# Attention decode step with a gated GLU: the last row of wo in two column halves, with the closing sums on GpSimd and VectorE

## The chip, the cores and the metric

The kernel runs on one core of a Trainium2 chip. The metric is the device time of one execution in microseconds. The engines are TensorE (PE in the profile; PEld is its weight load), VectorE (DVE), ScalarE (ACT), GpSimd (POOL) and SyncE (SP, which here only issues transfers). Sixteen DMA engines move data between the main memory (HBM) and the on-chip memory SBUF. TensorE writes its results to PSUM, from which VectorE and ScalarE read.

## The reference

One token `x` of 512 numbers is normalised. It then goes two ways: through attention over a cache of 8192 positions with 32 heads of 128 numbers, and through a gated unit whose silu is multiplied onto the attention's result. Everything is float32. Cut to what matters:

```python
# A: D = 512, H = 32, Sk = 8192, Dh = 128;  B: F = 1376
xn = layernorm(x)
q = (xn @ wq).reshape(1, 1, H, Dh)
p = softmax(einsum("bhqd,bhkd->bhqk", q, k_cache) * Dh ** -0.5)
s = einsum("bhqk,bhkd->bhqd", p, v_cache) -> (1, 1, H * Dh) @ wo      # wo: 4096 x 512
h = sigmoid(xn @ w_gate) * (xn @ w_up)
g = silu(h @ w_down)
out = x + s * g
```

The two caches hold 128 MB each (in units of 2 to the 20th), wq and wo 8 MB each.

## The kernel before

**Main part.** The 32 heads are worked off as 16 pairs. SP loads the keys of a pair (8 MB) into one of two slots in turn and the values into a third slot. VectorE multiplies the keys by the query in place (L415) and sums them to scores (L416). TensorE finds the largest score with ScalarE's and VectorE's help, ScalarE takes the exponentials (L430), and TensorE multiplies them by the values. Its instructions for one pair are recorded in a list by the class `Later` and played in a loop; each of them has the line L38 in the profile, so they are told apart by their tiles. The order on each engine is the order in which the program is written, with explicit semaphores: `wait(engine, step)` puts a wait ahead of the engine's next instruction, and `pe`, `dve`, `act` and `pool` count an engine's finished steps.

**Start.** VectorE clears `x_row` (L239). ScalarE's queue loads `x` into it (L240), 128 numbers on each of the partitions 0, 32, 64 and 96; these are the four groups (`NG` = 4, `GC` = 128 columns to a group). From `x_row` VectorE makes the normalised `xn`. GpSimd sets up constants with a few memsets and one select (L244 to L251), and clears a rest of w_down's place later (L323); after that it has nothing to do.

**Gate.** `column_sums` (L327) sums the rows of the gated unit's result over all partitions by matmuls with a column of ones. Each matmul puts 128 columns on the first partition of one group. ScalarE takes the sigmoid into `g_row` (L373). In the second turn of the pairs' loop VectorE multiplies `g_row` by the sum itself (L458), which completes silu.

**End.** `wo` is loaded by SP in nine pieces of rows (`W_ENDS`, L483; the profile names the line of the helper, L168). Row r of the 32 stands for 128 of the 4096 rows of wo, one on each partition, so a piece of one row is 128 runs of 2 KB. The rows are shared out as follows:

- rows in `W_DVE`: VectorE multiplies each by its column of `o_all`, the attention's output, and adds them into two partial sums (L513, L515), then adds those (L518);
- rows in `W_PE`: TensorE multiplies them into the bank `big[0]`, and VectorE adds this to its own sum, into `s_tmp` (`to_fold`, L490);
- rows 28 to 31 (`direct`): TensorE multiplies each, as soon as it has landed, in four matmuls of 128 columns into `acc`, one for each group of partitions. Ahead of row 31 it also sums `s_tmp` over the partitions into the same place (`fold`).

A matmul in float32 leaves two matmul records and two weight loads in the profile. At last VectorE multiplies `g_row` by `acc` (L537) and adds `x_row` (L539), and SP stores the four groups, 512 bytes each (L562), clears the semaphores and waits for the store to land.

## Time and profile before

| | |
|---|---|
| median of 3 runs | 684.65 us (684.42 to 684.74) |
| the profiled execution | 684.69 us |
| its span, first to last instruction | 683.3 us |
| mean granted TensorE clock | 0.67 |
| data read from HBM | 293.67 MB, 430 GB/s over the span |

How to read the profile: the page begins with the span and each engine's busy time and share. Then come rows with one digit for each of 40 equal slices of the span (9 is 90% busy or more). A row of an engine's groups has line, engine, operation, output<-inputs, shapes and count, then the busy time in us and the mean ns of one, then the engine's idle time before them in us and what ended it. In the timeline a row has start, length in us, engine and operation, and in brackets the idle time before it and what ended that; several instructions in a row are merged (x4), and the length is then from the first one's start to the last one's end. The chain of waits has start, length and what ran. A row for a DMA queue has its packets, the MB they moved and the share of the sixteen engines' time. SPq and ACTq are the engines' own queues, where they issue transfers.

### The profile page before, as it was taken

Reading aid. Unit: us, or ns where it says so; the run is one execution under the profiler, and the core shown is the slowest. Engines: PE = TensorE matmul, PEld = TensorE weight load, DVE = VectorE, ACT = ScalarE, POOL = GpSimd, SP = SyncE. Lnnn points to the kernel's source line nnn. Section 1 sums busy time; section 2 is a strip of 40 time slices with the busy share of each in tenths; the row PEclk is TensorE's granted clock in tenths of the full one; section 3 lists DMA queues with packets and bytes.
Section 4 is the critical chain, followed back from the end, with each engine's and each line's share of the span. In section 5 each row is a group of like instructions: output and inputs, shape, how many; then the busy total and the mean of one; then the engine's idle time right before and its main releaser. Section 6 shows DMA issues by size and latency. Waiting matters only on the chain. (4 is left out here: it accounts for less than half of the span.)

```text
span 683.3 us, 3400 instructions
## 1 busy us (share of the span) xinstructions
PE 218.8 (32%) x1376; PEld 62.3 (9%) x1376; DVE 616.0 (90%) x156; ACT 44.6 (7%) x142; POOL 2.6 (0%) x11
## 2 busy tenths in 40 slices
PE   0363025050503305050512306060512406060665
PEld 0120001010100101010100101010100101010110
DVE  3869999999999999998989899898989999999917
ACT  2040010000000100000010100000010101000010
POOL 0000000000000000000000000000000000000000
PEclk9987557575755757575665757575665757575897
DMA  9999999999999999999999999999999999999997
GB/s 382 429 440 460 437 434 430 430 430 430 430 430 430 430 430 430 460 441 445 434 430 430 430 430 430 430 430 430 430 437 437 460 430 403 472 399 430 435 430 331
DMA packets 7552, 293.67 MB, mean 430 GB/s; under 512 B 856, under 2 KB 864, under 8 KB 1664
## 3 DMA queue, kind: packets, MB, share of 16 engines
q1 hardware_dynamic: 7544, 293.67, 99.5%
q10 hardware_dynamic: 8, 0.00, 0.0%
HBM read 293.67 MB, written 0.00 MB: 430 GB/s over the span
## 5 line engine op out<-in xcount | busy, mean ns | idle before, releaser
L415 DVE TENSOR_TENSOR slot<-slot,q_all 128x16384 f32<-128x16384 f32 (+3 forms) x19 | 275.9, 14520 | 19.9 <-DMA slot<-in_A_k_cache_dram 19.9
L416 DVE TENSOR_REDUCE sc<-slot 128x128 f32<-128x16384 f32 (+3 forms) x19 | 276.0, 14525 | 0.7
L38 PE MATMUL psum<-slot,zeros 128*8 128x512 f32 x1024 | 148.5, 739 | 253.6 <-PEq L38 253.6
L38 PEld LDWEIGHTS psum<-slot,zeros 128*8 128x8 f32 x1024 | 30.3, 103 | 358.2 <-issue 358.2
L38 PE MATMUL psum<-ident,mx 128*1 128x128 f32 x32 | 8.4, 360 | 114.3 <-PEq L38 114.3
L437 ACT COPY o<-psum 128x512 f32<-128x512 f32 x16 | 9.4, 586 | 400.1 <-PE psum L38 400.1
L38 PE MATMUL psum<-slot,ones 128*128 (+3 forms) x36 | 17.7, 668 | 22.1 <-PEq L38 16.6
L290 DVE SCALAR_TENSOR_TENSOR slot<-slot,xn 128x1376 f32<-128x1376 f32 (+1 forms) x8 | 18.9, 2360 | 3.0 <-DMA slot<-in_A_wq_dram 2.7
L38 PE MATMUL psum<-o,pick 128*2 128x128 f32 x128 | 16.5, 272 | 12.8 <-PEq L38 12.8
L423 DVE STREAM_TRANSPOSE psum<-psum 32x128 f32<-32x128 f32 x16 | 5.0, 310 | 11.1 <-PE psum L38 11.1
L428 ACT ACTIVATE nb<-psum 128x2 f32<-128x2 f32 x16 | 2.8, 172 | 156.1 <-PE psum L38 156.1
L430 ACT ACTIVATE zeros<-sc,nb 64x128 f32<-64x128 f32 x32 | 12.8, 399 | 0.9
L38 PEld LDWEIGHTS psum<-ident,mx 128*1 128x1 f32 x32 | 1.8, 80 | 118.4 <-issue 118.3
L38 PEld LDWEIGHTS psum<-o,pick 128*2 128x2 f32 x128 | 9.9, 84 | 29.6 <-issue 27.2
L38 PE MATMUL psum<-slot,o_all 128*1 128x128 f32 (+1 forms) x54 | 9.5, 463 | 6.5 <-DMA slot<-in_A_wo_dram 6.5
L38 PE MATMUL psum<-zeros,rs 128*32 128x2 f32 x32 | 3.7, 187 | 23.5 <-PEq L38 23.5
L408 DVE TENSOR_REDUCE mx<-psum 1x2 f32<-1x128 f32 x16 | 4.4, 277 | 7.5 <-PE psum L38 7.5
L38 PE MATMUL psum<-mx,ones 1*128 1x2 f32 x32 | 8.2, 324 | 7.4 <-PEq L38 7.4
L515 DVE SCALAR_TENSOR_TENSOR q_all<-slot,o_all,q_all 128x512 f32<-128x512 f32 x15 | 10.0, 747 | 0.0
L38 PEld LDWEIGHTS psum<-slot,ones 128*128 128x128 f32 (+1 forms) x36 | 7.0, 218 | 32.5 <-issue 24.7
L38 PE MATMUL psum<-slot,o 128*1 128x512 f32 x26 | 5.0, 827 | 11.2 <-DMA slot<-in_B_w_down_dram 11.2
L38 PEld LDWEIGHTS psum<-mx,ones 1*128 1x128 f32 x32 | 7.3, 282 | 14.0 <-issue 14.0
(54 smaller groups left out, 61.3 us busy)
## 6 DMA issues: line engine op xcount, KB each, us to landing
slot<-in_A_k_cache_dram SPq DMA_DIRECT2D x2, 6144.0 KB, 37.9
slot<-in_A_v_cache_dram SPq DMA_DIRECT2D x3, 4096.0 KB, 23.0
slot<-in_A_wq_dram SPq DMA_DIRECT2D x2, 4096.0 KB, 16.6
slot<-in_A_k_cache_dram SPq DMA_DIRECT2D x2, 4096.0 KB, 40.5
slot<-in_A_k_cache_dram SPq DMA_DIRECT2D x2, 2048.0 KB, 42.4
slot<-in_B_w_gate_dram SPq DMA_DIRECT2D x1, 2752.0 KB, 26.9
slot<-in_B_w_up_dram SPq DMA_DIRECT2D x1, 2752.0 KB, 33.0
slot<-in_B_w_down_dram SPq DMA_DIRECT2D x1, 2560.0 KB, 22.7
```

The source lines that it names most:

```text
L38: ins = getattr(self.engine, name)(*args, **kwargs)
L290: return dve(DVE.scalar_tensor_tensor(y, w[:, k, cols], xn[:, k:k + 1], y, op0=ALU.mult, op1=ALU.add))
L408: DVE.reduce_max(mx[:1, 1:3], pt[0:1, :].rearrange("o (e p) -> o e p", e=2), axis=AX.X).then_inc(reduced, 1)
L415: wait(DVE, dve(DVE.tensor_mul(k[:, j, :], k[:, j, :], qb[:, i:i + 1, :].to_broadcast([P, n, Dh]))))
L416: summed[i] = dve(DVE.reduce_sum(sc[i % 2][:, j], k[:, j, :], axis=AX.X))
L423: turned_out[i] = dve(DVE.transpose(o, pn.rearrange("e (a r) -> e a r", r=WR)))
L428: wait(ACT, act(ACT.mul(nb, pm[:, :2], -SCALE)))
L430: ACT.activation(weights[h, :, e * HT:(e + 1) * HT], sc[i % 2][h].rearrange("p (g b) -> p g b", b=HT), AF.Exp, bias=nb[h, e:e + 1], scale= ...
L437: ACT.copy(o1, po).then_inc(copied, 1)
L515: ins = DVE.scalar_tensor_tensor(part[n], wo_t[:, r, :], col, part[n], op0=ALU.mult, op1=ALU.add)
```

## The change

The last row of wo, row 31, is loaded as two transfers of 256 columns each (128 runs of 1 KB), so there are ten pieces. All products of the rows 28 to 31 and of `s_tmp` are made by halves: eight matmuls of 64 columns in place of four of 128, into two banks, `acc[0]` and `acc[1]`. TensorE waits for each half of row 31 by itself. A group's 128 columns are now 64 of the first half of the result and 64 of the second. For that the gate's sums (`column_sums`), the stored result and a second load of `x` follow the new order. This second load goes into a new tile `x_add`, cleared at the start by VectorE and loaded on ScalarE's queue in the second turn of the pairs' loop; `x_row` stays as it was for the normalisation. VectorE multiplies the gate by the first half's product and GpSimd adds `x_add`; of the second half VectorE does both. SP waits for GpSimd and for VectorE, and stores eight runs of 256 bytes. There are two semaphores more.

```diff
--- before.py
+++ after.py
@@ -93,7 +93,7 @@
     W_DVE = [r for r in range(W_FOLD) if r not in W_PE]
     V_CUTS, K_CUTS = (NB // 2, NB * 13 // 16), {NP - 3: (NB * 3 // 4,), NP - 2: (NB * 3 // 4,), NP - 1: (NB // 2,)}
 
-    N_SEMS = 40
+    N_SEMS = 42
     DVE, ACT, SP, POOL = nc.vector, nc.scalar, nc.sync, nc.gpsimd
     PE = Later(nc.tensor)
     pe_only = OrderedEngineSet([nc.tensor.engine])
@@ -116,7 +116,7 @@
 
     pick = sb("pick", 2 * HT)
     slots = [sb(f"slot{i}", SLOT) for i in range(3)]
-    x_row, g_row = sb("x_row", GC), sb("g_row", GC)
+    x_row, g_row, x_add = sb("x_row", GC), sb("g_row", GC), sb("x_add", GC)
     ones, ident = sb("ones", P), sb("ident", P)
 
 
@@ -138,7 +138,8 @@
     psum = bank("psum", P, NK * QT)
     banks = [psum[:, i * QT:(i + 1) * QT] for i in range(NK)]
     big, po, wide = banks[:2], banks[2], banks[3:]
-    acc, pt, o_t = wide[0][:, :GC], wide[1][:, :P], wide[2][:GP, :H * WP + Dh]
+    pt, o_t = wide[1][:, :P], wide[2][:GP, :H * WP + Dh]
+    acc = [wide[n][:, :GC // 2] for n in range(2)]
     pm, pn = wide[3][:, :4], wide[4][:GP, :Dh]
 
 
@@ -238,6 +239,7 @@
 
     c_xrow = dve(DVE.memset(x_row, 0.0))
     ld_xr = load(ACT, "xr", x_row[0:P:GP, :], xv.rearrange("(g c) -> g c", g=NG), c_xrow)
+    c_xadd = dve(DVE.memset(x_add, 0.0))
     ACT.nop().then_inc(q_free, NK)
     ACT.nop().then_inc(s_val[1], 16 * (NP - 2))
     ACT.nop().then_inc(s_val[2], 16 * (NP - 1))
@@ -326,7 +328,8 @@
 
     def column_sums(dst, src):
         for g in range(NG):
-            ins = PE.matmul(dst[g * GP:g * GP + 1, :GC], ones[:, 0:1], src[:, g * GC:(g + 1) * GC], start=True, stop=True)
+            ins = PE.matmul(dst[g * GP:g * GP + 1, :GC].rearrange("r (h c) -> r h c", h=2), ones[:, 0:1],
+                            src.rearrange("p (h g c) -> p g h c", h=2, g=NG)[:, g], start=True, stop=True)
         return pe(ins)
 
     rows = []
@@ -456,6 +459,8 @@
         if i == 1:
             wait(DVE, c_sig)
             c_gate = dve(DVE.tensor_mul(g_row, g_row, big[1][:, :GC]))
+            ld_xa = load(ACT, "xa", x_add[0:P:GP, :].rearrange("g (h c) -> g h c", h=2),
+                         xv.rearrange("(h g c) -> g h c", h=2, g=NG), c_xadd)
     all_max(NP - 1)
     powers_of(NP - 1)
     wait(DVE, parts(NP - 1))
@@ -479,22 +484,21 @@
 
 
     wo_t = slots[NP % 2 ^ 1].rearrange("p (r e) -> p r e", e=D)
-    ld_o = []
+    ld_o, halves = [], (slice(0, D // 2), slice(D // 2, D))
     for n, (r0, r1) in enumerate(zip((0,) + W_ENDS, W_ENDS)):
-        ld_o.append(load(SP, f"wo{n}", wo_t[:, r0:r1, :], wo.rearrange("(p r) e -> p r e", r=WR)[:, r0:r1, :],
-                         summed[NP - 2] if n == 0 else None))
+        for c in halves if r1 == WR else (slice(0, D),):
+            ld_o.append(load(SP, f"wo{n}_{c.start}", wo_t[:, r0:r1, c], wo.rearrange("(p r) e -> p r e", r=WR)[:, r0:r1, c],
+                             summed[NP - 2] if n == 0 else None))
 
 
     def to_fold(after):
         wait(DVE, after, t_part)
         return dve(DVE.tensor_add(s_tmp, part[0], big[0]))
 
-    def fold(dst, copied, last):
-
-        wait(PE, copied)
+    def into_groups(n, col, row, **flags):
         for g in range(NG):
-            ins = PE.matmul(dst[g * GP:g * GP + 1, :GC], ones[:, 0:1], s_tmp[:, g * GC:(g + 1) * GC],
-                            start=last, stop=last)
+            c = slice(halves[n].start + g * GC // 2, halves[n].start + (g + 1) * GC // 2)
+            ins = PE.matmul(acc[n][g * GP:g * GP + 1, :], col, row[:, c], **flags)
         return ins
 
     piece = {r: ld for ld, *ends in zip(ld_o, (0,) + W_ENDS, W_ENDS) for r in range(*ends)}
@@ -525,18 +529,25 @@
                         start=(k < NG), stop=(k + NG >= len(W_PE)))
     folded = to_fold(pe(ins))
     direct = list(range(W_FOLD, WR))
-    for r in direct:
+    for r in direct[:-1]:
         landed(PE, r, direct)
-        for g in range(NG):
-            ins = PE.matmul(acc[g * GP:g * GP + 1, :], o_all[:, r:r + 1], wo_t[:, r, g * GC:(g + 1) * GC],
-                            start=(r == W_FOLD), stop=(r == WR - 1))
-        if r == WR - 2:
-
-            fold(acc, folded, False)
-    wait(DVE, pe(ins))
-    t = dve(DVE.tensor_mul(g_row, g_row, acc))
-    wait(DVE, t)
-    t = dve(DVE.tensor_add(g_row, g_row, x_row))
+        for n in range(2):
+            into_groups(n, o_all[:, r:r + 1], wo_t[:, r, :], start=(r == W_FOLD), stop=False)
+    wait(PE, folded)
+    for n in range(2):
+        into_groups(n, ones[:, 0:1], s_tmp, start=False, stop=False)
+    summed_out = []
+    wait(DVE, ld_xa)
+    wait(POOL, ld_xa)
+    for n, ld in enumerate(ld_o[-2:]):
+        wait(PE, ld)
+        ins = into_groups(n, o_all[:, WR - 1:], wo_t[:, WR - 1, :], start=False, stop=True)
+        wait(DVE, pe(ins))
+        y = g_row[:, n * GC // 2:(n + 1) * GC // 2]
+        t = dve(DVE.tensor_mul(y, y, acc[n]))
+        add, done = ((POOL, pool), (DVE, dve))[n]
+        wait(add, t)
+        summed_out.append(done(add.tensor_add(y, y, x_add[:, n * GC // 2:(n + 1) * GC // 2])))
     after = PE.take()
 
 
@@ -549,7 +560,7 @@
         PE.play(each)
     PE.play(after)
 
-    wait(SP, ld_o[-2])
+    wait(SP, ld_o[-3])
     nc.regs_alu(once, once, 1, op=ALU.add)
     for e in (ACT, DVE, PE.engine, POOL, SP):
         br = e.br_lt(once, 1, on_true="body", on_false="leave")
@@ -558,8 +569,9 @@
     body.close()
     nc.switch_bb("leave")
 
-    wait(SP, t)
-    SP.dma_start(out.rearrange("a b (g c) -> (a b g) c", g=NG), g_row[0:P:GP, :]).then_inc(s_out, 16)
+    wait(SP, *summed_out)
+    SP.dma_start(out.rearrange("a b (h g c) -> (a b g) h c", h=2, g=NG),
+                 g_row[0:P:GP, :].rearrange("g (h c) -> g h c", h=2)).then_inc(s_out, 16)
 
 
     used = sorted(s.num for s in sems)
```

## The prediction

> **What bounds the kernel now.** I read the page first: the span, the busy shares, the DMA rows.
>
> ```profile
> span 683.3 us, 3400 instructions
> ...
> PE 218.8 (32%) x1376; PEld 62.3 (9%) x1376; DVE 616.0 (90%) x156; ACT 44.6 (7%) x142; POOL 2.6 (0%) x11
> ...
> DMA  9999999999999999999999999999999999999997
> ...
> q1 hardware_dynamic: 7544, 293.67, 99.5%
> ```
>
> The SP queue q1 fills 99.5% of the sixteen DMA engines' span. The kernel streams 293.67 MB, and only the slice after the last byte is not full. The change moves no byte out of this stream, so it can win only in the tail. The chain of waits shows that tail; its last rows, with start, length and what ran:
>
> ```profile
> 650.58 28.68 DMA slot<-in_A_wo_dram
> ...
> 679.29 1.23 PE psum L38 x32
> ...
> 680.54 0.44 PE psum L38 x8
> ...
> 681.00 0.30 DVE g_row L537
> 681.30 0.02 issue
> 681.33 0.29 DVE g_row L539
> ```
>
> The chain follows TensorE back from 680.54 to 679.29. The timeline corrects this:
>
> ```profile
> 678.05 0.09 PEld L38 LDWEIGHTS psum<-slot,o_all 128*1 128x1 f32 x4 [1.20 <-DMA slot<-in_A_wo_dram]
> ...
> 679.12 0.69 DVE L490 TENSOR_TENSOR q_all<-q_all,psum 128x512 f32<-128x512 f32 x1 [0.65 <-PE psum L38]
> 679.29 0.32 PEld L38 LDWEIGHTS psum<-slot,o_all 128*1 128x1 f32 x16 [1.15 <-DMA slot<-in_A_wo_dram]
> ...
> 679.90 0.11 PEld L38 LDWEIGHTS psum<-slot,o_all 128*1 128x1 f32 x8 [0.29 <-DMA slot<-in_A_wo_dram]
> ...
> 680.12 0.40 PE L38 MATMUL psum<-q_all,ones 128*1 128x128 f32 x8
> 680.54 0.11 PEld L38 LDWEIGHTS psum<-slot,o_all 128*1 128x1 f32 x8 [0.31 <-DMA slot<-in_A_wo_dram]
> ...
> 681.65 0.63 SPq L562 DMA_DIRECT2D out_dram<-g_row  x1
> ```
>
> Each weight load with a wait in brackets is a piece of wo that has just landed: rows 28 and 29 at 679.29, row 30 at 679.90, row 31 at 680.54. So row 31 is waited for too, by 0.31 us. From there to the span's end are 2.8 us: 0.46 to the product, 0.65 on VectorE to SP's issue, and 1.65 (681.65 to 683.3) for the store, which the change does not shorten. What can be won lies within the first 1.1 us, 0.16% of the time.
>
> **The change part by part.** Most of the tail's sum hangs on what half the columns cost.
>
> ```profile
> 678.48 0.60 PE L38 MATMUL psum<-slot,o_all 128*1 128x512 f32 x2
> ```
> ```profile
> 680.12 0.29 PE L38 MATMUL psum<-q_all,ones 128*1 128x128 f32 x4
> ```
> ```profile
> 680.23 0.29 PE L38 MATMUL psum<-q_all,ones 128*1 128x128 f32 x4
> ```
> ```profile
> L490 DVE TENSOR_TENSOR q_all<-q_all,psum 128x512 f32<-128x512 f32 x1 | 0.7, 687 | 0.6 <-PE psum L38 0.6
> ...
> L38 PE MATMUL psum<-q_all,ones 128*1 128x128 f32 x8 | 0.4, 272 | 0.0
> ...
> L539 DVE TENSOR_TENSOR g_row<-g_row,x_row 128x128 f32<-128x128 f32 x1 | 0.3, 292 | 0.0
> L537 DVE TENSOR_TENSOR g_row<-g_row,psum 128x128 f32<-128x128 f32 x1 | 0.3, 289 | 1.2 <-PE psum L38 1.2
> ...
> L469 DVE TENSOR_TENSOR psum<-psum,den 32x32 f32<-32x32 f32 x1 | 0.2, 187 | 0.0
> ```
>
> TensorE. The program gives each product as two matmul records, and four products (the groups) stream side by side: four begin within 0.02 us (0.29 less the mean of 0.272) and the next four 0.11 later. I call that a round. 512 columns take 0.60 and 128 take 0.272, 0.85 ns a column, so a round is nearly all columns. At 64 columns I take 0.055 for a round and 0.272 - 64 x 0.00085 = 0.218 for a record. The tail has ten rounds now (40 records: 32 on o_all, 8 on the sum) and twenty after, of half the length, so its stream stays at 1.1 us. The bounds: 0.055 a round, or no gain at all, 0.11; I take the lower end, since the two lengths shown lie on one line through nearly nothing.
>
> VectorE. From 687 at 512 columns and 289 at 128, 1.04 ns a column: 289 - 66 = 223 ns at 64. The 32-column row at 187 sits on that line (289 - 99 = 190). So 0.22 for each product and 0.225 for its add; bounds 0.19 (the 32-column row) and 0.29.
>
> The load of row 31 in two. What one more transfer costs is seen at the pieces: two rows as one piece took 679.29 - 678.05 = 1.24, two rows as two pieces 680.54 - 679.29 = 1.25. What smaller packets cost comes from the DMA rows of two stretches of 1.0 and 0.7 us, first of 6 KB packets, then of 2 KB:
>
> ```profile
> q1 hardware_dynamic: 67, 0.41, 96.6%
> ```
> ```profile
> q1 hardware_dynamic: 150, 0.28, 103.8%
> ```
>
> The first: 0.966 x 16 x 1.0 / 67 = 231 ns a packet. The second holds 0.28 MB, about 137 packets of 2 KB with a few of semaphores: 1.038 x 16 x 0.7 / 137 = 85 ns. The line through both has 73 ns for 2 KB and 12 for the packet, so eight more packets on each engine are 0.1 us. Bounds 0 and 0.1; I take 0.05. The second half then lands in time for 680.59, the first at about 679.90 + 0.64 / 2 + 0.02 = 680.24.
>
> SP's queue issues one transfer more.
>
> ```profile
> 647.73 10.98 SPq L168 DMA_DIRECT2D slot<-in_A_wo_dram  x9
> ```
> ```profile
> L168 SPq DMA_DIRECT2D slot<-in_A_wo_dram x9: 430/432/4160, 647.7 to 655.3; - x9
> ```
>
> Nine issues end at 658.7, the last two held up (up to 4.16 us). A tenth held up as long ends at 662.9. Its data are not due before 680.2, so 17 us cover it; were the cover gone, it would cost its 0.43. The only work behind it on SP is its wait for row 30 and the store.
>
> **The tail summed.** Rows 28 and 29 start at 679.29 (8 short rounds, to 679.73), row 30 at 679.90 (4, to 680.12), and the sum at 680.12, which VectorE finished at 679.81 (4, to 680.34). The first half, there since 680.24, starts at 680.34, its last record at 680.34 + 0.055 + 0.02, and ends 0.218 later at 680.63. Before, VectorE began its product 0.46 after the first of row 31 (680.54 to 681.00), of which 0.11 + 0.02 + 0.272 = 0.40 were the matmuls, so it follows 0.06 after the last; this product runs from 680.69 to 680.91, hidden while the second half lands. The second half runs from 680.59 to 680.59 + 0.055 + 0.02 + 0.218 = 680.88; its product from 680.94 to 681.16; the add from 681.20 to 681.42 (gap 0.03 as between 681.30 and 681.33); SP's issue at 681.45 instead of 681.65. That is 0.20 us less.
>
> GpSimd's add of the first half. No GpSimd instruction with two inputs is in the trace; its own rows:
>
> ```profile
> L323 POOL MEMSET slot<- 128x1536 f32 x1 | 1.4, 1382 | 35.1 <-PE psum L38 35.1
> ...
> L248 POOL TENSOR_SCALAR_AFFINE_SELECT ident<-zeros 128x128 f32<-128x128 f32 x1 | 0.3, 292 | 0.2 <-POOL zeros L246 0.2
> ...
> L251 POOL MEMSET zeros<- 64x1 f32 x2 | 0.2, 92 | 0.1
> ```
>
> Bounds are 0.09 (one column) and 1.38 (1,536 columns). The nearest is the only one that reads: 0.29 at 128 columns. From 680.97 it ends at 681.26, 0.16 before VectorE's add, and costs nothing; at 1.38 it ends at 682.35, 0.93 after it. The SBUF — State Buffer page of the Trainium skill (section "Who interferes with whom") speaks against this pair: a VectorE instruction with both inputs in SBUF and a GpSimd instruction that reads SBUF exclude each other, and the later one waits in full. By it VectorE's add would begin at 681.26 instead of 681.20 and the gain would be 0.14, not 0.20; no run so far shows such a pair.
>
> The store has eight runs of 256 bytes instead of four of 512, and SP waits for two semaphores. The nearest row is the issue of 0.63 and the 1.02 from its end to the span's end. Bounds: nothing, and that 1.02 once more; I take 0.02.
>
> Edits that cost nothing, with their cover:
>
> ```profile
> 2.18 0.17 DVE L239 MEMSET x_row<- 128x128 f32 x1 [2.18 <-PEq L196]
> 9.10 0.40 DVE L260 STREAM_TRANSPOSE g_row<-x_row 128x128 f32<-128x128 f32 x1 [6.75 <-DMA x_row<-in_A_x_dram]
> ```
> ```profile
> 165.71 0.17 ACT L428 ACTIVATE nb<-psum 128x2 f32<-128x2 f32 x1 [16.89 <-PE psum L38]
> ```
> ```profile
> 67.45 0.40 PE L38 MATMUL psum<-slot,ones 128*1 128x128 f32 x8 [0.68 <-ACT slot L369]
> ```
> ```profile
> L168 ACTq DMA_DIRECT2D x_row<-in_A_x_dram x1: 1077/1077/1077, 2.4 to 2.4; - x1
> ```
>
> The memset of x_add (x_row's took 0.17) lies in VectorE's 6.75 us of waiting for x; bare it would cost 0.17. The second load of x (1.08 to issue) stands on ScalarE's queue ahead of the exponentials of the next pair, where ScalarE waits 16.89 us; bare, 1.08. Its 2 KB are 0.005 us of the stream. VectorE and GpSimd wait for it some 500 us later. The gate's sums in the new column order read two runs of 64 columns; were the 0.40 doubled, the next load of values would be issued 0.4 later into a queue whose slices there are full.
>
> Sum: -0.20 + 0.02 = -0.18 us. The profiled execution took 684.69 (span 683.3 and 1.39 around it), which gives 684.5; against the median of the runs, 684.65, 0.04 below it, 684.47. I say 684.5, 0.03% faster: about 0.2%, 1.37 us, is what a measurement of this kernel can tell from no change.
>
> **The rivals.**
>
> Small matmuls at the old pace. If a round stays 0.11, twenty take 2.2 us: 679.29 + 8 x 0.11 = 680.17, row 30 to 680.61, the sum to 681.05, the halves to 681.49, the last record's end at 681.62 instead of 680.94. That is +0.68; the shorter end on VectorE (0.51 in place of the 0.65) takes 0.14 off and the store adds its 0.02, +0.56: 685.2. Against it are the four starts within 0.02. The page TensorE: Matmul & The Clock Gate of the Trainium skill (Part 1, "Wait — 56ns, not 53.3ns?") gives a floor of about 25 ns between matmul starts, which by its figure would make a round of four 100 ns. The trace disagrees for matmuls on different groups: four starts in 0.02.
>
> The first half doesn't land earlier than the second. Then the first half starts at 680.59 too, its product at 680.94, and the second product (from 681.19) and the add (from 681.44) follow behind it on VectorE: SP issues at 681.70, +0.05, and with the store's 0.02 it is 684.7. Against it are the 0.61 and 0.64 between single rows, in order.
>
> The store dearer by its 1.02: -0.2 + 1.02, 685.5. Nothing in the trace writes 256 bytes. The page DMA: Bandwidth & Descriptors (section "Specifications") of the Trainium skill says that writes below 512 bytes are read, modified and written back, which points this way without a price.
>
> Slower: GpSimd's add sets the end. SP waits for it as well. It decides over 0.2% when the add ends after 681.62 + 1.37 = 682.99, that is when it takes over 2.0 us. It is this instruction's first use; the row nearest to a first-use price is ScalarE's table load:
>
> ```profile
> 3.71 1.28 ACT L254 ACT_TABLE_LOAD   x1 [3.71 <-issue]
> ```
>
> One such load and GpSimd's longest row make 1.28 + 1.38 = 2.66: the add ends at 683.63, +2.0 us, 686.7. With the load and 0.29 it would be 682.54, +0.9, 685.6, and not decide. For it: nothing hides it. Against it: the first select stood only 0.2 us behind the memset before it. The GPSIMD Engine Reference of the Trainium skill (section 2.1, "Instruction dispatch") gives about 6 µs for the first call into freshly loaded code; an estimate by it is about 690. The select's 0.2 does not show such a price.
>
> **How the numbers follow.** Forecast 0.75; old pace 0.07; halves together 0.07; dearer store 0.05; GpSimd late 0.04; 0.02 for what no row shows (x_add moves the tiles behind it by 512 bytes), half of it to each side. Over 0.2% slower are GpSimd and half the rest: 0.05. Faster by as much is 0.01, since the tail holds only 1.1 us to win; same 0.94. The range: low end 684.1, the forecast less 0.15 (the second half landing without the 0.05, products at 0.19) and less the runs' own 0.2 below their median; high end 685.3, with old pace and halves inside. Dearer store and GpSimd stay out, with the rest 0.11.
>
> **What the profile after will show.** The product's tail: matmuls of 64 columns in rounds of 0.05, the first half's product on VectorE done before the last weight load lands, two VectorE products near 0.22, a GpSimd add near 0.3 starting about 680.97, the store issued at 681.45. The prediction is wrong if rounds stay at 0.11, if GpSimd's add ends after VectorE's, if the store's part grows beyond 1.65, or if the stream's 99.5% falls.

## The result, and the profile after

The changed kernel takes 686.46 us, the median of 21 executions (685.68 to 688.16). The kernel before, beside it on the same chip, took 684.94 us, the median of 21 (684.39 to 685.78). The ratio is 1.0025, with a 95% interval of 1.0019 to 1.0031. So the change makes the kernel 0.25% slower. The forecast was 684.5, and its range ended at 685.3.

The profiled execution of the changed kernel took 687.32 us, 2.63 more than that of before. The page shows a queue that the page of before does not have. Its rows for queues give kind, packets, MB, and share of the sixteen engines' time:

```profile
span 685.9 us, 3488 instructions
...
GB/s 386 424 436 470 428 428 425 432 428 428 428 459 447 436 428 428 428 432 428 428 428 462 443 436 428 428 428 432 428 428 431 460 421 457 429 399 439 403 420 299
...
q1 hardware_dynamic: 7692, 293.67, 99.2%
q8 instruction: 1, 0.02, 0.0%
q10 hardware_dynamic: 20, 0.00, 0.0%
```

One packet of the kind "instruction" passed through the DMA engines. By the trace's own record it has 16,384 bytes, begins at 106.63 us and holds one engine for 0.93 us. It is so small that its share rounds to 0.0%, and it is what slows the kernel. To see why, look at how the loads land. The page's rows with forty slices can be asked for over 6 us, so that a slice is 0.15 us. From 125 to 131 us, before:

```profile
GB/s 0 0 0 0 0 0 0 2621 1748 2185 437 0 0 0 0 0 0 0 0 0 0 0 0 1748 2185 2621 437 0 0 0 0 0 0 0 0 0 0 0 0 1748
```

and after:

```profile
GB/s 0 0 0 0 0 1748 1311 1311 1748 437 0 0 0 0 0 437 0 0 0 0 0 1311 1748 874 2185 437 0 0 0 0 0 437 0 0 0 0 0 1311 1748 874
```

A packet is counted in the slice in which it begins, and one packet of 64 KB gives 437 in such a slice. A packet takes 2.42 us and the next turn comes 2.43 us later, so an engine begins a packet as it ends the last. Before, the sixteen engines begin their packets within four slices, then there is a gap until the next sixteen, 2.4 us later. After, fifteen begin together and one begins six slices (0.9 us) behind them, and again at the next turn. The same picture is there 300 us later (420 to 426 us, after):

```profile
GB/s 0 0 0 1311 2621 1311 1311 0 0 0 0 0 0 437 0 0 0 0 0 1311 2621 874 1748 0 0 0 0 0 0 437 0 0 0 0 0 874 3058 0 2621 0
```

One engine stays behind for over 500 us: by the trace's landing events, sixteen for a load, the last engine is 0.92 us behind the fifteenth at 121 us and 1.00 at 642 us. With 99.2% of the engines' time filled there is hardly a pause in which to make up 0.93 us. A load counts as landed when its last engine is done. After 642 us the picture changes, as shown below.

The tail of the changed kernel, from the timeline (start, length, what, idle time before it and what ended that):

```profile
681.89 0.44 PEld L38 LDWEIGHTS psum<-slot,o_all 128*1 128x1 f32 x32 [1.14 <-DMA slot<-in_A_wo_dram]
...
682.48 0.22 PEld L38 LDWEIGHTS psum<-slot,o_all 128*1 128x1 f32 x16 [0.15 <-DMA slot<-in_A_wo_dram]
...
682.70 0.41 PE L38 MATMUL psum<-q_all,ones 128*1 128x64 f32 x16
...
682.93 0.53 PE L38 MATMUL psum<-slot,o_all 128*1 128x64 f32 x16
683.36 0.39 DVE L547 TENSOR_TENSOR g_row<-g_row,psum 128x64 f32<-128x64 f32 x2 [0.94 <-PE psum L38]
683.74 0.32 POOL L550 TENSOR_TENSOR g_row<-g_row,x_add 128x64 f32<-128x64 f32 x1 [643.78 <-DVE g_row L547]
683.78 0.36 DVE L550 TENSOR_TENSOR g_row<-g_row,x_add 128x64 f32<-128x64 f32 x1
684.22 0.67 SPq L573 DMA_DIRECT2D out_dram<-g_row  x1
```

Row 28 and 29's weight load begins at 681.89 instead of 679.29, and everything follows 2.6 us later. By the trace's landing events the last part of row 31 is there at 683.12, against 680.50 before: +2.62. From there to SP's issue of the store it is 1.10 (before 1.15), from there to the span's end 1.73 (before 1.68), and around the span 1.37 (before 1.36; the trace has the two spans as 685.95 and 683.33). So 2.62 - 0.05 + 0.05 + 0.01 = 2.63: all of the loss is in the stream, and the tail is not where it went.

Of these 2.62, the lag explains about 1. The profiled execution belongs to the slower of two groups. The 21 spans fall into twelve from 684.3 to 685.1 (median 684.65) and nine from 685.5 to 686.8; the median span of before was 683.5 to 683.7 in the comparisons below. In this execution the other part has a place. At 642 us the last engine's landing is 0.82 later than before's, at 660 us 2.60; the first engine's is 0.17 earlier and then 0.75 later. Between the two, the distance from the last engine to the fifteenth falls from 1.00 to 0.48, while that from the last to the first grows from 1.48 to 2.37: it is no longer one engine alone that is late. The rows for 640 to 655 us, which is where the loads change from the caches to wo, give the busy time of each engine with the number of instructions, then the granted clock, the DMA share and the GB/s. Before, after, and the changed kernel with both closing sums on VectorE, whose one execution was another of that group (experiment 7):

```profile
640.00:655.00 15.00, 9.84 (x62) 2.79 (x66) 11.08 (x10) 1.89 (x7) 0.00 (x0) 0.78 0.98 423
```
```profile
640.00:655.00 15.00, 8.64 (x54) 2.48 (x58) 11.83 (x10) 1.89 (x7) 0.00 (x0) 0.80 0.97 388
```
```profile
640.00:655.00 15.00, 9.68 (x62) 2.86 (x66) 11.95 (x10) 1.89 (x7) 0.00 (x0) 0.77 0.94 364
```

The DMA engines are nearly as busy as before but move 388 and 364 GB/s instead of 423. 35 GB/s less over 15 us are 0.53 MB, which at 423 GB/s take 1.2 us. The packets themselves are longer: of 32 KB up to 2.04 us and of 20 KB up to 1.41, where before's take 1.21 and 0.76 without exception. A smaller dip is also in a kernel without the packet, that with four idle matmuls of experiment 1 (its span was 683.9):

```profile
640.00:655.00 15.00, 9.68 (x62) 2.78 (x66) 11.00 (x10) 1.89 (x7) 0.00 (x0) 0.76 0.96 411
```

### The profile page after: what moved, and what is told of

Same layout as the page of the kernel before. It is cut to its first block, busy times and chain, and to the rows that moved or that the text cites. A ratio compares the mean times of both kernels' runs of the same rounds, so it can differ in the third digit from the quotient of the medians.

```text
span 685.9 us, 3488 instructions
## 1 busy us (share of the span) xinstructions
PE 223.1 (33%) x1416; PEld 62.9 (9%) x1416; DVE 616.7 (90%) x158; ACT 44.6 (6%) x142; POOL 2.9 (0%) x12
## 3 DMA queue, kind: packets, MB, share of 16 engines
q1 hardware_dynamic: 7692, 293.67, 99.2%
## 5 line engine op out<-in xcount | busy, mean ns | idle before, releaser
L38 PE MATMUL psum<-slot,zeros 128*8 128x512 f32 x1024 | 150.3, 746 | 254.7 <-PEq L38 254.7
L38 PE MATMUL psum<-slot,o_all 128*1 128x64 f32 (+1 forms) x86 | 11.1, 389 | 5.1 <-DMA slot<-in_A_wo_dram 5.1
```

The source lines that it names most:

```text
L38: ins = getattr(self.engine, name)(*args, **kwargs)
```

## The experiments

The theory: the change makes TensorE's program longer, by twenty matmuls; that passes a limit beyond which 16 KB of instructions are fetched while the kernel runs, by one of the sixteen DMA engines, in the middle of a saturated stream. One rival: the loss is in what the change does on purpose (halves, the second load of x, GpSimd's sum). Another: it is the fetch as such, TensorE's pause or its clock. The expectations give them letters, and say in words which they mean. The spans in the table are medians of the faster group; the landing is that of the last part of row 31 in the profiled execution; "behind" is the distance of the last engine from the fifteenth near 580 us.

| kernel | median us | ratio to before, 95% | instruction packet | behind, us | row 31 landed | faster group: executions, span |
|---|---|---|---|---|---|---|
| changed kernel | 686.46 | 1.0025 [1.0019, 1.0031] | 106.6 us | 0.94 | 683.12 | 12 of 21, 684.65 |
| before + 4 matmuls | 685.01 | 1.000 [0.9991, 1.001] | none | 0.05 | 681.11 | 10 of 10, 683.6 |
| before + 7 | 687.88 | 1.0045 [1.003, 1.0061] | 685.3 us, after the span | 0.08 | 680.26 | 4 of 4, 683.5 |
| before + 10 | 686.62 | 1.0025 [1.0014, 1.0036] | 107.0 us | 1.28 | 682.23 | 5 of 9, 684.5 |
| before + 20 | 687.05 | 1.003 [1.0018, 1.0042] | 106.8 and 684.1 us | 1.03 | 682.03 | 3 of 6, 684.8 |
| changed, no second load of x | 686.84 | 1.0028 [1.0016, 1.004] | 104.4 us | 1.03 | 681.67 | 3 of 6, 684.5 |
| changed, 20 matmuls less elsewhere | 685.83 | 1.0011 [1.0002, 1.002] | none | 0.07 | 680.50 | 11 of 11, 684.4 |
| changed, 16 matmuls less elsewhere | 684.87 | 0.9999 [0.999, 1.0008] | none | 0.08 | 680.24 | 11 of 11, 683.5 |
| before + load of 61 x 32 B | 685.15 | 1.0016 [1.0004, 1.0028] | none | 0.50 | 680.76 | 9 of 12, 683.7 |
| before + load of 61 x 256 B | 685.68 | 1.0017 [1.0008, 1.0026] | none | 0.75 | 681.07 | 7 of 11, 683.9 |
| before + load of 61 x 512 B | 687.16 | 1.0033 [1.002, 1.0046] | none | 1.0 | 682.95 | 2 of 5, 685.1 |
| before + load of 61 x 1024 B | 742.98 | (696.77 to 760.66) | none | 2.5 | 738.58 | 0 of 6 |

**1. Idle matmuls: is it the length of the program?** Behind the main part of before's program, where TensorE has time, matmuls are added whose result nothing uses:

```diff
+    for k in range(20):            # 10, 4 and 7 in the other kernels
+        g = k % NG * GP
+        PE.matmul(acc[g:g + 1, :GC // 2], ones[:, 0:1], ident[:, :GC // 2], start=True, stop=True)
```

Twenty:

> The kernel before, with 20 more matmuls of 64 columns on TensorE, placed in its idle time just ahead of the wait for the attention's output; row 31, the gate's order, x and the closing sums stay as before. Theory A (TensorE's program has grown past what is loaded at the start, so one 16 KB piece of instructions is fetched while the stream runs, and the one DMA engine that carries it stays about 1 us behind the others to the end): these 20 matmuls add as many instructions as the change added, so a row of instructions appears beside the DMA queues at about 106 us, the last landings fall some 1.0 us later, and the time is 0.9 to 1.5 us above before: 685.9 to 686.4. Theory B (the halves of row 31, the second load of x or GpSimd's add cost the time): nothing of them is here, so 684.9, no instruction row.

Ten:

> The kernel before with 10 more matmuls of 64 columns at the same place, half as many. Theory A: if the limit is at 512 instructions and the kernel before has about 430 of them on TensorE, 40 more stay below it: no fetch, 684.9. Were the limit lower than that, a fetch and 685.9. Theory B: 684.9. A cost in proportion to the matmuls themselves would be half of that of the run with 20.

Four:

> The kernel before with 4 more matmuls (16 instructions) on TensorE instead of 10 or 20. It looks for the limit: if before has 16 instructions to spare there is no fetch and 684.9; if not, a fetch at about 106 us and 685.9 or more. Any version of the halves needs at least 4 more matmuls.

Seven:

> The kernel before with seven idle matmuls of 64 columns added in TensorE's idle time, 28 instructions by the trace's count of four for one: between four (no instruction packet, 1.000) and ten (one packet, 1.0025). Theory A: the time follows the packet, 685.0 without it, 685.7 or more with it, and nothing between. Rival (the cost grows with the number of matmuls): about half of the ten's, 685.8, with or without the packet.

With ten and with twenty, nothing of the change is there, and the time is that of the changed kernel (1.0025 and 1.003). Both medians lie above what was expected with a packet, since about half of the executions are in a slower group, and the room for 40 more instructions that the expectation for ten counted on was not there. With four the time is that of before. The DMA rows with twenty and with four:

```profile
q1 hardware_dynamic: 7544, 293.67, 99.3%
q8 instruction: 2, 0.03, 0.0%
q10 hardware_dynamic: 8, 0.00, 0.0%
```
```profile
q1 hardware_dynamic: 7544, 293.67, 99.4%
q10 hardware_dynamic: 8, 0.00, 0.0%
```

So the time follows the packet. Seven went by a way that no theory had: the span is that of before (683.5) and the store is issued at 681.41, but the time is 687.88. The time around the span is 4.1 to 4.7 us instead of 1.3 to 1.6. Rows of 683 to 690 us show why:

```profile
DMA packets 1, 0.02 MB, mean 2 GB/s; under 512 B 0, under 2 KB 0, under 8 KB 0
...
q8 instruction: 1, 0.02, 0.8%
```

The packet comes after the last instruction of the span, alone on the engines, and the kernel's time is some 2.9 us longer than before's with the same span. The reading that fits is that between four and seven matmuls, that is 16 and 28 instructions at four records for a matmul, the program's end crosses the limit, and that between seven and ten the fetch moves into the stream, where it costs less. The second packet of the twenty, at 684.09, is of the same kind: three of its six executions had 2.2 to 2.4 us around the span. (One execution each of the changed kernel and of the ten had 2.4 to 2.5, and one of before's beside them 2.1; why is not shown.)

**2. The change without one of its parts.** The second load of x is left out, and both sums read `x_row`, so that x is added in the old order of columns:

```diff
-        summed_out.append(done(add.tensor_add(y, y, x_add[:, n * GC // 2:(n + 1) * GC // 2])))
+        summed_out.append(done(add.tensor_add(y, y, x_row[:, n * GC // 2:(n + 1) * GC // 2])))
```

> The changed kernel without the second load of x and its tile: the closing sums add the first load of x, so x is added in the wrong order of columns. TensorE's program is that of the change. Theory A: the fetch stays, 686.0 to 686.5. Theory C (the second load of x, on ScalarE's queue, is what disturbs the stream): 684.8 to 685.0. This run also shows whether the slower stretch of the stream from 640 to 655 us in the change's trace comes again; if it belongs to the change it should be here, if it is an accident of that one execution it should not.

1.0028, with the packet: the second load is not the loss. The median of 686.84 is above the 686.5 expected, with three of six executions in the slower group. The profiled one is of the faster group, and it answers the question about 640 to 655 us: all its packets from 642 to 654 us take 1.21 and 0.76 us as before, and the last engine stays behind to the end (1.03 at 652 us, 1.09 at the last landing). So the longer packets are not in every execution of the change's program.

**3. The change without the longer program.** Matmuls are left out elsewhere, and with them parts of the gate and of the attention's output, so that TensorE's program is as long as before's. First twenty are left out, seven of them from the row products of wo (`W_PE` cut to four rows):

> The changed kernel with as many matmuls fewer on TensorE as the change added, taken from elsewhere: 9 of the 13 products with w_down, one column sum of the gated unit, 3 of the 4 selecting matmuls of each pair and 7 of the 11 products in W_PE are left out, so the gate and the attention's output are not the reference's. Loads, halves of row 31, second load of x, closing sums and store are those of the change. Theory A (the fetch of instructions): no fetch, landings within 0.5 us of each other, and 684.8 (684.6 to 685.0), so that the change without its fetch is level with before or 0.1 to 0.2 faster. Theory B (halves, small packets, second load, GpSimd, store): 686.0 to 686.5 as the change.

There was no packet, and the landings were on time (680.50, before's value). The time was still 0.11% above before's, but the loss was in another place: the clock granted from 676 to 682 us was 0.50 (the last number but two of the row), against 1.00 in the row of the next kernel. That it comes from the missing row products fits, since from 670 to 676 us TensorE has no matmul here and 5.05 us of them in the next kernel; it was not tested apart.

```profile
676.00:682.00 6.00, 5.19 (x88) 2.57 (x88) 3.16 (x6) 0.00 (x0) 0.00 (x0) 0.50 0.67 262
```

The small matmuls ran late at that clock and SP issued the store at 682.78. The kernel had changed two things at once. So the row products were left whole, and sixteen other matmuls taken:

```diff
-            ins = PE.matmul(d[:, :c.stop - c.start], ones, src[:, 0, c], start=True, stop=True)
+            if c.start == 0:
+                ins = PE.matmul(d[:, :c.stop - c.start], ones, src[:, 0, c], start=True, stop=True)
...
-    for c in range(FP + FC):
+    for c in range(NG):
...
-        for b in range(HT):
+        for b in range(1):
```

> The changed kernel with sixteen matmuls left out elsewhere (nine of the thirteen of the w_down product, four of the six column sums of the gated unit, three of the four that select columns in each head pair), the row-by-row work on wo kept whole, so that TensorE's program is four matmuls longer than before's, as in the run with four idle ones added, which had no instruction packet. Theory A (the loss is the fetch of one 16 KB block of instructions): no packet on the instruction queue, the last landing of row 31 within 0.2 us of before's, a granted clock in the tail of 1.00 as in before, and the time is that of a tail shortened by 0.05 to 0.2 us: 684.8 (684.6 to 685.0). Rival B (the loss is in the halves themselves, the second load of x, or GpSimd's addition): 686.0 or more, without the packet.

684.87, ratio 0.9999 [0.999, 1.0008], eleven executions from 684.46 to 685.11, none in a slower group. Its rows:

```profile
q1 hardware_dynamic: 7692, 293.67, 99.5%
q10 hardware_dynamic: 20, 0.00, 0.0%
```
```profile
676.00:682.00 6.00, 3.66 (x90) 1.28 (x88) 3.58 (x8) 0.00 (x0) 0.32 (x1) 1.00 0.64 250
```
```profile
680.87 0.32 POOL L551 TENSOR_TENSOR g_row<-g_row,x_add 128x64 f32<-128x64 f32 x1 [641.37 <-DVE g_row L548]
680.90 0.37 DVE L551 TENSOR_TENSOR g_row<-g_row,x_add 128x64 f32<-128x64 f32 x1
681.35 0.67 SPq L574 DMA_DIRECT2D out_dram<-g_row  x1
```

All of the change is in this kernel: halves, GpSimd's sum, the second load, the store of eight runs. Without the packet it costs nothing that can be measured, and gains nothing. This rules out the rival of the parts, and it settles the first half of the theory.

**4. The lag without a fetch: which step of the packet costs?** To load one engine with about 1 us and fetch nothing, before gets one more load on ScalarE's queue, 61 runs of 256 bytes, which all went through one engine (the load has a single packet of 4 bytes, the semaphore's, where the second load of x has four). The first form made ScalarE wait for it in the fourth turn:

```diff
+            ld_extra = load(ACT, "extra", extra[:61, :], wq[:61, :64])
+        if i == 3:
+            wait(ACT, ld_extra)
```

> The kernel before with one small load more and no more instructions on TensorE: in the second turn of the pairs' loop ScalarE's queue loads 256 bytes onto each of 61 partitions, 16 KB in all, into a tile that nothing reads. If all of it is carried by one DMA engine, as I expect of 61 runs, that engine loses 61 times about 18 ns (the 256-byte packets of the change's second load of x), 1.1 us. Theory A, its second half (what one engine loses in the full stream is not made up, and the last landing is late by it): no instruction row, one landing of each load about 1 us behind the other fifteen from 120 us on, time 685.7 to 686.1. Rival: what costs the time is the fetch as such (the sequencer waiting), not the engine's lag: 684.9. If the lag is enough to bring the second, slower group of times (about 687.5, seen in half of the runs of the kernels with a fetch and hardly in those of before), it will show here too.

This was a failed experiment: 699.85 us. The load took far longer than a few us, and ScalarE stood still meanwhile: in the profiled execution it was issued at 146.88 us, its last packet ended at 187.9, and ScalarE's next copy, at 195.14, followed 39.8 us of idle time. Five executions took 698 to 700 us; the profiled one took 869.7, at a granted clock of 1.00, and why is not shown. So the time holds the wait, and the lag cannot be read from it. The second form has no wait in the stream, only one of SP's at the end:

```diff
+            ld_extra = load(ACT, "extra", extra[:61, :], wq[:61, :64])
...
-    wait(SP, ld_o[-2])
+    wait(SP, ld_extra, ld_o[-2])
```

> The kernel before, and in the second turn of the pair loop one more load from ScalarE's queue, 61 runs of 256 bytes, about 16 KB on one DMA engine, for which nobody waits before the end of the program. It loads the engine with about the time of the instruction block (0.93 us by the profile of the changed kernel) and fetches no instructions. Theory A, second half (time that one engine of sixteen loses in the saturated stream is not made up, and every later load ends with its last landing that much later): one landing of every later load about 1.1 us behind the other fifteen, 685.7 to 686.1. Rival C (it is the fetch as such, TensorE standing still or its clock): 684.8 to 685.1 in spite of the lost time. If the times above 687 that the kernels with the packet had in part come from the lag alone, some of these runs are there too.

Its trace shows why the load is long. The 61 packets did not go one after the other: one, at times two, stood between two 64 KB packets of q1, 2.43 us apart, so that the load lasted from 114 to 245 us. From 420 to 426 us there is the same picture as with the packet:

```profile
GB/s 0 0 0 437 3495 1311 1311 0 0 0 0 437 0 0 0 0 0 0 0 437 3495 874 1748 0 0 0 0 437 0 0 0 0 0 0 0 0 3932 874 1748 0
```

One engine is behind by 0.75 us, not the 1.1 expected. An explanation that fits, but was not tested, is that the rest went into the place that the engine had within the usual spread of 0.5 us. The ratio is 1.0017 [1.0008, 1.0026], and the median of 685.68 lies at the lower end of what the theory expected, but only as a median over two groups: seven executions have spans of 683.6 to 684.3 (median 683.9, 0.2 above the 683.7 of before in that comparison), four of 685.7 to 686.2. So a lag of one engine, with no fetch, no longer program and no pause of TensorE, gives a loss, and gives the two groups as well. In the faster group the loss is smaller than the lag. The rival of TensorE's pause is not needed: this kernel has before's TensorE program.

**5. How the loss grows with the lag.** The same load with longer and shorter runs.

1024 bytes:

> As the kernel with the extra load of 61 runs for which nobody waits, but each run of 1024 bytes instead of 256, so that the one DMA engine loses more. The 256-byte runs took 18 ns each (1.1 us together) and the 512-byte runs of x 27 ns, so 1024 bytes are estimated at 45 ns and the load at 2.7 us of one engine. With 256 bytes the last landing of row 31 came 0.57 us later than before's and the undisturbed group of times was near 685.4. Theory A (what one engine loses in the saturated stream is not made up, and the end moves with it): the last landing 1.4 to 2.7 us later than before's, the time in proportion, 686.4 to 687.7. Rival (the stream gives such time back, and the 256-byte load cost its 0.4 us by something else): no more than with 256 bytes, 685.4.

32 bytes and 512 bytes:

> The extra load of 61 runs for which nobody waits, with runs of 32 bytes. From 4 bytes in 9 ns and 256 bytes in 18 ns a run is estimated at 10 ns, the load at 0.6 us of one engine, half of the 256-byte load. Theory A (one engine out of step costs its own delay, and past about 1 us at times the rate of the whole stream): 685.1 to 685.4, and no execution above 686.5. Rival (the group above 687 comes with any load in the middle of the stream, whatever its size): about a third of the executions above 686.5.

> The same load with runs of 512 bytes, 27 ns each by the loads of x, 1.65 us of one engine, between the 256-byte load (0.75 us behind, median 685.68, 4 of 11 above 687) and the 1024-byte load (2.5 us behind, 697 to 761). Theory A (the stream's rate falls past some distance between the engines): most executions above 687, and the more so the longer the rate stays low, 687 to 700. Rival (each engine's delay is only its own, and the 1024-byte load's 743 us have another cause): 686.0 to 686.6, with no more above 687 than with 256 bytes.

The distance behind grew as expected: 0.50, 0.75, 1.0 and 2.5 us. So did the faster group's span: 683.7, 683.9 and 685.1, though not in proportion. The 1024-byte load went far beyond every expectation: all six executions took 697 to 761 us. Rows for 300 to 500 us, before and with this load, when the load itself was long over (its last packet ended by 254 us):

```profile
300.00:500.00 200.00, 61.53 (x422) 17.57 (x413) 183.02 (x26) 10.03 (x36) 0.00 (x0) 0.64 1.00 435
```
```profile
300.00:500.00 200.00, 56.13 (x390) 15.92 (x390) 163.58 (x25) 9.44 (x35) 0.00 (x0) 0.63 1.00 388
```

The DMA engines are busy all the time in both, but the whole stream moves 388 GB/s instead of 435. Every 64 KB packet in this stretch takes 2.71 us, against 2.42 before (and 2.42 with the 32-byte and 512-byte loads). So one engine out of step by 2.5 us does not only end late; with it all the packets become longer. The rival, that each engine's delay is only its own, falls there. But the theory in the form that the rate falls only past about 1 us falls too: with the 32-byte load and a lag of 0.5 us no execution was to be above 686.5, and three of twelve took 688.05 to 688.4, near the third that its rival had expected. With 512 bytes three of five are above 687, the other two at 686.46 and 686.64, so that run does not decide between its two expectations.

**6. What stays open.** A lag of one engine, whether by a fetch or by a load, brings a second group of executions, 1 to 3 us above the first. In the kernels with neither it is rare: with four idle matmuls 10 of 10 and with sixteen matmuls less 11 of 11 were in the faster group, and of before's 86 executions whose spans are known beside the experiments three had a span above 684.4. These three (684.5, 684.7 and 684.8) are all among the 16 beside the ten and twenty idle matmuls, where before's median was 683.6. So an execution can be longer without a lag that the program brings. Which executions fall into the second group, and why the packets between 640 and 655 us become longer there, no run shows.

**7. GpSimd's sum beside VectorE's.** Both closing sums on VectorE:

```diff
-        add, done = ((POOL, pool), (DVE, dve))[n]
+        add, done = DVE, dve
...
-    wait(SP, *summed_out)
+    wait(SP, summed_out[-1])
```

First in the kernel with twenty matmuls less:

> The run without 20 matmuls elsewhere (gate and attention's output not the reference's), and with both closing sums on VectorE instead of the first on GpSimd. One look at the tail. If GpSimd's add holds up VectorE's (in the change it took 0.356 us where 0.22 was forecast, while GpSimd's ran), the second add takes 0.22 here and SP issues the store no later than in the run with GpSimd; if 0.356 is what an add of two inputs in SBUF costs, it stays.

then in the changed kernel itself:

> The changed kernel with both closing additions on VectorE and none on GpSimd. If GpSimd's addition holds up VectorE's (0.356 us in the changed kernel beside 0.22 to 0.23 for the other VectorE instructions of that size), each addition takes 0.22 to 0.23 us here and SyncE issues the store 0.95 to 1.05 us after the last landing of row 31 instead of 1.09. If the 0.356 us have another cause, the last addition stays at 0.35. The instruction packet stays, so the time is that of the changed kernel, 685.6 to 687.5.

The second one's rows:

```profile
683.79 0.22 DVE L546 TENSOR_TENSOR g_row<-g_row,psum 128x64 f32<-128x64 f32 x1 [0.95 <-PE psum L38]
684.04 0.22 DVE L549 TENSOR_TENSOR g_row<-g_row,x_add 128x64 f32<-128x64 f32 x1
684.19 0.21 DVE L546 TENSOR_TENSOR g_row<-g_row,psum 128x64 f32<-128x64 f32 x1
684.43 0.23 DVE L549 TENSOR_TENSOR g_row<-g_row,x_add 128x64 f32<-128x64 f32 x1
684.69 0.67 SPq L572 DMA_DIRECT2D out_dram<-g_row  x1
```

Alone, VectorE's sum takes 0.22 to 0.23 us (0.22 and 0.23 in the first kernel too), beside GpSimd's 0.32 it takes 0.36 to 0.37. So GpSimd's instruction holds up VectorE's by 0.13 to 0.15. The second part of the expectation missed: SP issues 1.15 after the last landing (683.54), not 0.95 to 1.05, because VectorE now has four instructions one behind the other. The two arrangements are worth the same within 0.06 us. The kernel's 687.8 us, in one execution, is that of the changed kernel's slower group and above the 687.5 expected. The first kernel took 686.51 in one execution, with a span of 684.1 and a packet at 685.3, after the span, as with seven matmuls. TensorE's program there is that of the kernel with twenty matmuls less, which had no packet; only VectorE's, GpSimd's and SP's differ. So TensorE's program is not all that can bring such a packet, and whose this one was, the trace does not say.

No version beat the kernel before. The best that the change can be, with the program kept short, is experiment 3's 684.87 against 685.03, inside its interval; so no version that shortens TensorE's program and keeps the reference's result was measured.

## Why the prediction was wrong

**The step that failed** stands in its first part: "The change moves no byte out of this stream, so it can win only in the tail." That is true of the kernel's own loads, and it asks only what can be won. What can be lost was looked for in the tail, in the queues and on GpSimd, but twenty more matmuls were costed only by the time in which they run. They are also some 80 more instructions in TensorE's program, and that brought a transfer of 16 KB into the stream. The row that was quoted, 99.5% of sixteen engines, already said that any new transfer has no cover. Not one rival has this mechanism, and the 0.02 "for what no row shows" was all the chance that it had. The same question was asked for the second load of x, whose 2 KB were costed at 0.005 us, as a mean over sixteen engines. That did no harm there, but the packet shows that the mean is the wrong number, since it loads one engine: 0.93 us, not 0.93 / 16 = 0.06. What stays open is the rest of the loss, the longer packets between 640 and 655 us in the slower group.

The page "Runtime: NRT & Kernel Launch" of the Trainium skill (section "Instruction fetch mechanics") says that an engine's instructions are refilled in blocks of 16 KiB over a DMA queue of the sequencer, and calls the cost of a boundary "mostly hidden". The trace agrees on the block's size; here it costs about 1 us of span (684.65 against 683.6) in the faster group alone.

**The tail, point by point.**

- Rounds of four matmuls: predicted 0.055 for 64 columns, and a record 0.218. The four rounds of the folded sum take 0.41 (predicted 3 x 0.055 + 0.02 + 0.218 = 0.40). Right: the rival "small matmuls at the old pace" is out.
- The first half's product was to be done before the last weight load lands. It was not: the two VectorE products run from 683.36 to 683.75, and the second half landed at 683.12. It cost nothing, though. The second half's last matmul ends at 683.46 by the trace, and VectorE's second product begins 0.07 later, as predicted (0.06). The halves landed 0.34 us apart (682.78 and 683.12; predicted 0.35), so the rival in which they land together is out.
- VectorE's instructions of 64 columns: predicted 0.22, found 0.22. Its sum beside GpSimd's: predicted 0.225, found 0.36. This term was mis-sized by 0.13. This is where the page SBUF — State Buffer of the Trainium skill (section "Who interferes with whom") spoke against the pair, by its rule on two inputs; the trace agrees that there is a price, 0.13. Had the whole sum waited for GpSimd's, it would have ended at 683.74 + 0.32 + 0.22 = 684.28; it ended at 684.14. In three kernels (this one and the two of experiment 3 with GpSimd's sum) VectorE's sum ends 0.08 after GpSimd's. In that of experiment 2 VectorE's began when GpSimd's had 0.09 left, and took 0.22. So a wait to GpSimd's end that holds only the last part of VectorE's instruction fits all four; no run tests it.
- GpSimd's sum: predicted 0.29, found 0.318, with no price of first use. The rival with the opposite sign was out, though its number for the time (686.7) came near by another way.
- The store: issue to the end of the span 1.73 instead of 1.68, predicted +0.02. Near; in the kernel with sixteen matmuls less it is 1.73 too. SP's issue begins 0.08 after VectorE's sum ends (684.14 to 684.22), where 0.03 was predicted.
- Sum of the tail: predicted -0.18. Found from the last landing to the end of the span: 1.10 + 1.73 = 2.83, against 1.15 + 1.68 = 2.83, so nothing. The gain in matmuls and VectorE's shorter products is there; VectorE's slowed sum (0.13), SP's start (0.05) and the store took it back. In the kernel of experiment 2, where GpSimd's sum had begun 0.23 before VectorE's, SP issued 0.97 after the last landing and the whole tail was 2.70, 0.13 less than before.

So two things were wrong. The small one, in the tail, would have left the time inside the stated range: experiment 3 gives 684.87. The large one is the fetch.

"The prediction is wrong if the stream's 99.5% falls" was the right thing to watch: it fell to 99.2%. The number alone is a weak sign, though: the kernel with twenty matmuls less, which had no packet, has 99.3%.

## What to carry to other kernels

In a kernel that fills its DMA engines, look at the number of instructions that a change adds to an engine, not only at the time in which they run: near a limit, sixteen to forty more instructions bring a 16 KB fetch, and the DMA rows of the page show it as a queue of the kind "instruction". Cost a small transfer in a saturated stream by what it takes of its one engine, not by the mean over sixteen, and expect the whole stream to end later: in the faster groups here by about 1 us for an engine 0.94 to 1.28 us behind and by 0.2 for one 0.75 behind, in the slower ones by 1 to 3 us more. Experiments that add work should be made with the parts apart: idle instructions alone showed in one run that the change's purpose had nothing to do with the loss.

## What the runs showed that was not expected

- The limit of TensorE's program here lies between 16 and 28 instructions above before's. At 28 the fetch came after the last instruction and cost 2.9 us of time that is outside the span; from 40 up it came at 104 to 107 us, and cost 1 us or more inside.
- An engine once behind stayed behind for over 500 us of a saturated stream: 1.00 us at 642 us, after 0.93 us lost at 107. Only in the kernel without the second load of x was it so to the end (1.09); in the others with a packet the distance changed between 642 and 660 us.
- With one engine 2.5 us out of step the rate of all of them was 388 instead of 435 GB/s and each 64 KB packet took 2.71 instead of 2.42 us, long after the load that caused it; the executions took 697 to 761 us against 685.
- Packets of a second queue did not pass together: on their engine one, at times two, went between two 64 KB packets of q1, 2.43 us apart, so that 61 packets of 18 ns took 130 us to land.
- With less work for TensorE ahead of the tail, the clock granted in the tail was 0.50 instead of 1.00, and the time was 1.0011 of before's in spite of landings on time.
